# Accumulating the o and dq sums of four heads in one PSUM bank: an attention-and-MLP backward kernel on one core

## The chip, the cores and the metric

The kernel runs on 1 core of one Trainium2 chip. The metric is device time in microseconds (us) of one execution. Each kernel was timed in several rounds, alternating with the kernel before on the same chip; the tables give the median of a kernel's runs. The granted clock is the share of PE's full clock that the profile says PE was given.

The engines are named as in the profile: PE (matrix products), PEld (PE's weight loads, which overlap PE), DVE (vector engine), ACT (scalar engine), POOL, SP (which issues the large transfers), and DMA (the core's 16 DMA engines).

## The reference, cut to what matters

One token passes through a layer norm, 32-head attention over a cache of 8192 keys and values per head, and a small gated MLP. The kernel returns the output and all gradients, among them those of the whole K and V cache.

```python
# per head: k, v are [8192, 128] bf16; q, do (gradient of o) are [128]
scores = (k @ q) * 128 ** -0.5
p  = softmax(scores)
o  = p @ v                      # "o sum"
# backward, as jax.vjp derives it
dp = v @ do
ds = p * (dp - sum(p * dp))
dq = ds @ k                     # "dq sum"
dv = outer(p, do)               # 2 MB per head, stored
dk = outer(ds, q)               # 2 MB per head, stored
```

Per head 2 MB of K and 2 MB of V are loaded and 2 MB of each gradient are stored: 4 x 2 MB x 32 heads = 268 MB of the 304 MB that move in all.

## The kernel before: the parts that the change touches

The order of all instructions is fixed by hand. A head's K and V tiles are transposed on PE (`T`, copied out by ACT), multiplied with q and do (`Mp`), turned into two rows of 64 columns by "select" products (`selm`), put through softmax, and then summed (`wsum`) and used for the outer products (DVE), which overwrite the tiles before they are stored.

```python
ps_t = ctx.enter_context(tc.tile_pool(name="ps_t", bufs=4, space=PSUM))   # transposes AND sums
...
def wsum(h, kind, pair):                 # kind "V": o sum, kind "K": dq sum
    N4 = 4 * DH
    W = kv_tiles[(kind, h)]
    X = pst()                            # one of the 4 transpose banks
    for i in range(J // 4):              # 16 products of 32 columns
        q = QW * (i % 4)
        nc.tensor.matmul(X[q:q + QW, :], lhsT=pair[:, 4 * i:4 * i + QW, 0], rhs=W[:, N4 * i:N4 * (i + 1)],
                         start=(i < 4), stop=(i >= J // 4 - 4), skip_group_check=True)
    XS = kt_tile()
    nc.scalar.copy(XS[:].rearrange("p k w -> p (k w)"), X[:])          # ACT, twice per head
    hd[h]["xs" + kind] = XS

def col(h, kind):                        # twice per head, one head later
    ...
    for r in range(4):                   # "mask products": f32
        nc.tensor.matmul(S_["m"][:, OC + a:OC + a + 1], lhsT=XS[:, r, :], rhs=mask4[:, r:r + 1],
                         start=False, stop=(r == 3), skip_group_check=True)
    if a:
        nc.scalar.copy(grp[g]["od"][:, hh, :], S_["m"][:, OC:OC + 2])

def store(kind, h):
    t = kv_tiles.pop((kind, h))
    ...
    fifo((dkc if kind == "K" else dvc)[h], t[:])     # SP issues the store
    free_slots.append(t)
    load_next()                                      # and then the next load into a free tile
```

Loads and stores of the K and V tiles all go through one queue, issued by SP in program order. Ten tiles circulate.

## Time and profile before

| kernel before | us |
|---|---|
| median of 6 runs (first comparison) | 738.7 (736.96 to 740.21) |
| span of the profiled execution | 735.9 |

The first excerpt is from the profile page of the kernel before: busy time and share of each engine with the number of its instructions, three lines of the DMA queues (packets, MB, share of the 16 engines' span), and the chain of waits by engine, that is, the chain of work that ended last, followed back from the end.

```profile
PE 639.8 (87%) x6143; PEld 464.7 (63%) x6143; DVE 446.7 (61%) x745; ACT 402.5 (55%) x796; POOL 29.9 (4%) x45
...
q1 hardware_dynamic: 21328, 276.39, 89.3%
q0 software_dynamic: 5728, 26.30, 8.9%
q8 instruction: 48, 0.79, 0.4%
...
PE 64%; DMA 12%; DVE 10%; ACT 8%; issue 3%; ACTq 0%; SPq 0%; DVEq 0%
```

PE is the busiest engine and has most of the chain, which by itself says "PE is the bound". The table of stretches says otherwise. Its columns are: stretch and length in us, busy time (and instructions) of each engine, granted PE clock, share of the DMA engines' time, GB/s moved.

```profile
100.00:200.00 100.00, 92.35 (x893) 67.83 (x893) 56.71 (x95) 60.40 (x122) 2.94 (x4) 0.95 1.01 415
200.00:300.00 100.00, 93.70 (x897) 66.43 (x896) 64.04 (x97) 59.16 (x122) 4.91 (x6) 0.93 1.01 424
300.00:400.00 100.00, 93.48 (x923) 68.28 (x923) 63.25 (x99) 61.02 (x125) 4.02 (x5) 0.97 1.01 425
400.00:500.00 100.00, 93.08 (x888) 67.19 (x886) 64.56 (x100) 59.67 (x122) 3.27 (x4) 0.95 1.01 425
500.00:600.00 100.00, 93.66 (x876) 66.62 (x874) 64.13 (x97) 59.01 (x121) 4.13 (x5) 0.93 1.01 426
600.00:680.00 80.00, 74.00 (x691) 53.62 (x692) 49.77 (x76) 46.97 (x95) 1.63 (x2) 0.94 1.01 428
```

The DMA share is 1.01 in every stretch (it exceeds 1 because a packet's record overlaps the next one's). PE is 93% busy beside it: two things run at almost the same pace, and which one sets the time must be read from who waits. The groups that the change touches (line, engine, operation, output<-input, count | busy us, mean ns | idle time before, and what ended it):

```profile
L423 PE MATMUL m<-masks,KT 128*128 128x1 f32 x512 | 70.2, 259 | 0.0
L398 PE MATMUL pT<-kv,U 128*32 128x512 bf16 x512 | 46.2, 497 | 0.9 <-DVE U L411 0.9
L401 ACT COPY KT<-pT 128x512 f32<-128x512 f32 x64 | 38.7, 605 | 28.9 <-PE pT L398 28.7
L358 PE MATMUL m<-ident_f,mrow 128*128 128x128 f32 x64 | 12.4, 275 | 0.0
L293 PE MATMUL pT<-ident_f,kv 128*128 128x128 f32 x2048 | 311.3, 291 | 5.9 <-DMA kv<-in_A_k_cache_dram 4.0
L328 PE MATMUL m<-selc,KT 128*128 128x16 f32 x512 | 68.0, 265 | 29.3 <-ACT KT L318 29.2
```

The transposes (L293) are the first PE work on a tile, and before them PE stood idle for K and V loads 5.8 us in the whole run. The kernel before is thus hardly ever out of data; it only stays in step with the loads.

### The profile page before, as it was taken

How to read it: one execution, taken by the hardware profiler on the slowest of the kernel's cores; microseconds unless marked ns; L12 is line 12 of the kernel's file. 1: busy time of each engine (PE TensorE's matmuls, PEld its weight loads, DVE VectorE, ACT ScalarE, POOL GpSimd, SP SyncE). 2: the span in 40 equal slices, each digit the busy share in tenths (PEclk: the TensorE clock that was granted, in tenths of full speed). 3: DMA queues.
4: the chain of work that ended last, by engine and by line, in shares of the span. 5: the costliest groups of instructions: out<-in, count | busy, mean ns of one | idle time of the engine just before them, and what ended most of it. 6: DMA issues, size and time to landing. Idle time of an engine off the chain costs nothing.

```text
span 735.9 us, 14854 instructions
## 1 busy us (share of the span) xinstructions
PE 639.8 (87%) x6143; PEld 464.7 (63%) x6143; DVE 446.7 (61%) x745; ACT 402.5 (55%) x796; POOL 29.9 (4%) x45
## 2 busy tenths in 40 slices
PE   1999679999999999999999999999999999989950
PEld 1667457676667666766666666766666666666630
DVE  4057765666556666667656656676666655566482
ACT  1660646565656565665565655666565556655610
POOL 0010010000000000000000000000000000000000
PEclk9995799998999999999999999999999999989965
DMA  9999999999999999999999999999999999999993
GB/s 338 401 409 421 425 430 423 391 413 410 428 420 423 428 427 426 417 426 428 430 417 425 430 427 426 419 431 425 427 419 427 428 428 429 425 429 429 424 391 150
DMA packets 27432, 303.97 MB, mean 413 GB/s; under 512 B 2836, under 2 KB 4436, under 8 KB 10724
## 3 DMA queue, kind: packets, MB, share of 16 engines
q1 hardware_dynamic: 21328, 276.39, 89.3%
q0 software_dynamic: 5728, 26.30, 8.9%
q8 instruction: 48, 0.79, 0.4%
q10 hardware_dynamic: 308, 0.33, 0.1%
q14 instruction: 20, 0.16, 0.1%
HBM read 151.67 MB, written 151.34 MB: 412 GB/s over the span
## 4 chain that ended last, share of the span: by engine, by line
PE 64%; DMA 12%; DVE 10%; ACT 8%; issue 3%; ACTq 0%; SPq 0%; DVEq 0%
PE pT L293 27%; PE m L328 8%; PE m L423 7%; DMA kv<-in_A_k_cache_dram 7%; PE sA L312 6%; PE pT L398 5%; ACT KT L295 4%; DVE kv L430 4%; DMA kv<-in_A_v_cache_dram 4%; PE dA L312 2%; DVE side L239 2%; ACT KT L318 2%; DMA wo_g<-in_A_wo_dram 2%; PE gu_ps L507 1%; PE m L372 1%
## 5 line engine op out<-in xcount | busy, mean ns | idle before, releaser
L295 ACT COPY KT<-pT 128x512 f32<-128x512 f32 x512 | 292.0, 590 | 185.6 <-PE pT L293 100.9
L293 PE MATMUL pT<-ident_f,kv 128*128 128x128 f32 x2048 | 311.3, 291 | 5.9 <-DMA kv<-in_A_k_cache_dram 4.0
L293 PEld LDWEIGHTS pT<-ident_f,kv 128*128 128x128 f32 x2048 | 245.8, 153 | 49.8 <-PE pT L293 17.5
L430 DVE TENSOR_TENSOR kv<-qd,U 128x4096 bf16<-128x4096 bf16 x64 | 146.0, 2284 | 0.0
L430 DVE TENSOR_TENSOR kv<-qd,P 128x4096 bf16<-128x4096 bf16 x64 | 143.5, 2283 | 0.0
L328 PEld LDWEIGHTS m<-selc,KT 128*128 128x128 f32 x512 | 62.3, 192 | 49.5 <-ACT KT L318 44.8
L328 PE MATMUL m<-selc,KT 128*128 128x16 f32 x512 | 68.0, 265 | 29.3 <-ACT KT L318 29.2
L423 PEld LDWEIGHTS m<-masks,KT 128*128 128x128 f32 x512 | 65.0, 200 | 15.4 <-issue 15.4
L354 DVE TENSOR_REDUCE mrow<-m 128x1 f32<-128x64 f32 x32 | 7.2, 225 | 106.4 <-PE m L328 106.4
L423 PE MATMUL m<-masks,KT 128*128 128x1 f32 x512 | 70.2, 259 | 0.0
L312 PE MATMUL sA<-KT,qz 128*32 128x512 bf16 x512 | 56.0, 427 | 0.0
L401 ACT COPY KT<-pT 128x512 f32<-128x512 f32 x64 | 38.7, 605 | 28.9 <-PE pT L398 28.7
L312 PE MATMUL dA<-KT,qz 128*32 128x512 bf16 x512 | 53.6, 404 | 0.2 <-ACT KT L295 0.2
L387 DVE SCALAR_TENSOR_TENSOR U<-m,P 128x64 bf16<-128x64 f32 x32 | 7.4, 232 | 75.7 <-PE m L328 72.7
L312 PEld LDWEIGHTS <-qz 128*32 128x32 bf16 x1024 | 26.6, 93 | 41.4 <-issue 40.3
L398 PE MATMUL pT<-kv,U 128*32 128x512 bf16 x512 | 46.2, 497 | 0.9 <-DVE U L411 0.9
L398 PE MATMUL pT<-kv,P 128*32 128x512 bf16 x512 | 34.7, 387 | 0.0
L348 ACT CAST qd<-pT 128x256 bf16<-128x256 f32 x32 | 11.9, 372 | 41.4 <-DVE kv L430 32.7
L398 PEld LDWEIGHTS <-U 128*32 128x32 bf16 x512 | 15.9, 116 | 18.5 <-issue 11.9
L480 DVE SCALAR_TENSOR_TENSOR wq_g<-wq_g,side 128x512 bf16<-128x512 bf16 x40 | 27.3, 684 | 0.0
L361 DVE TENSOR_REDUCE negM<-m 128x1 f32<-128x128 f32 x32 | 9.3, 292 | 29.6 <-PE m L358 29.6
L239 DVE SCALAR_TENSOR_TENSOR side<-wo_g,g_bc 128x640 bf16<-128x640 bf16 x32 | 26.2, 820 | 1.6 <-DMA wo_g<-in_A_wo_dram 1.2
(144 smaller groups left out, 405.6 us busy)
## 6 DMA issues: line engine op xcount, KB each, us to landing
out_dram<-kv SPq DMA_DIRECT2D x64, 2048.0 KB, 28.8
kv<-in_A_k_cache_dram SPq DMA_DIRECT2D x32, 2048.0 KB, 25.6
kv<-in_A_v_cache_dram SPq DMA_DIRECT2D x32, 2048.0 KB, 25.8
out_dram<-wo_g POOLq DMA_DIRECT2D x8, 640.0 KB, 12.1
out_dram<-wq_g POOLq DMA_DIRECT2D x8, 640.0 KB, 13.1
wq_g<-in_A_wq_dram POOLq DMA_DIRECT2D x7, 640.0 KB, 14.0
wo_g<-in_A_wo_dram POOLq DMA_DIRECT2D x7, 640.0 KB, 19.7
kv<-in_B_w_dram SPq DMA_DIRECT2D x2, 1728.0 KB, 29.7
```

Of the source, the lines that this page charges most:

```text
L239: nc.vector.scalar_tensor_tensor(junk[:], G_["wo"][:, hh, :], 1.0, g_bc[:], ALU.mult, ALU.mult, accum_out=G_["do"][:, hh:hh + 1])
L293: nc.tensor.transpose(pT[:, k * P:(k + 1) * P], W3[:, 4 * c + k, :], ident_f[:])
L295: nc.scalar.copy(KT[:].rearrange("p k w -> p (k w)"), pT[:])
L312: nc.tensor.matmul(S_[kind][q:q + QW, :], lhsT=S_["qz"][:, o:o + QW], rhs=KTb[:, par, :], start=(c0 == 0), stop=(c0 == NCH - 2), skip_grou ...
L318: nc.scalar.copy(XS[:].rearrange("p k w -> p (k w)"), S_.pop(kind)[:])
L328: nc.tensor.matmul(S_["m"][:, b0:b0 + J].rearrange("p (c k t) -> p k c t", k=4, t=2)[:, k, :, :], lhsT=XS[:, k, :], rhs=selc[:].rearrange( ...
L348: nc.scalar.copy(qd[:].rearrange("p a d -> p (a d)"), hd[h].pop("ps_r"))
L398: nc.tensor.matmul(X[q:q + QW, :], lhsT=pair[:, 4 * i:4 * i + QW, 0], rhs=W[:, N4 * i:N4 * (i + 1)], start=(i < 4), stop=(i >= J // 4 - 4) ...
L401: nc.scalar.copy(XS[:].rearrange("p k w -> p (k w)"), X[:])
L423: nc.tensor.matmul(S_["m"][:, OC + a:OC + a + 1], lhsT=XS[:, r, :], rhs=mask4[:, r:r + 1], start=False, stop=(r == 3), skip_group_check=True)
L430: nc.vector.tensor_tensor(dst[:, lo * DH:hi * DH].rearrange("p (j a b) -> p j a b", a=DH // 2, b=2), vec.rearrange("p (a b) -> p a b", b=2 ...
L480: nc.vector.scalar_tensor_tensor(wq_g[:, ci, :], wq_g[:, ci, :], 1.0, dqb, ALU.mult, ALU.mult, accum_out=dxa[:, ci, g:g + 1])
```

## The change

The intent is less work per head on PE and ACT. The 16 products of each sum now read a buffer `Z` in which the values stand in four of every 32 columns; sliding the window by `4*slot` puts head and kind into their own four rows of each quarter. So eight sums (o and dq of four heads) accumulate in one PSUM bank, with one copy out and one set of mask products per four heads. The bank is taken from the transposes (four buffers become three), DVE fills `Z` twice per head, `P2`/`U2` become single, and the broadcast of the row maximum becomes a transpose.

```diff
-    ps_t = ctx.enter_context(tc.tile_pool(name="ps_t", bufs=4, space=PSUM))
+    ps_t = ctx.enter_context(tc.tile_pool(name="ps_t", bufs=3, space=PSUM))
+    ps_x = ctx.enter_context(tc.tile_pool(name="ps_x", bufs=1, space=PSUM))
 ...
+        nc.vector.tensor_copy(Z_vals, P2[:, :, 0].rearrange("p (i r) -> p i r", r=4))      # probs
 ...
+        nc.vector.tensor_copy(Z_vals, S_["U2"][:, :, 0].rearrange("p (i r) -> p i r", r=4)) # dsum
 ...
-    def wsum(h, kind, pair):
-        X = pst()
-        for i in range(J // 4):
-            nc.tensor.matmul(X[q:q + QW, :], lhsT=pair[:, 4 * i:4 * i + QW, 0], rhs=W[:, N4 * i:N4 * (i + 1)],
-                             start=(i < 4), stop=(i >= J // 4 - 4), skip_group_check=True)
-        nc.scalar.copy(XS[:].rearrange("p k w -> p (k w)"), X[:])
+    def wsum(h, kind, a):
+        slot = 2 * hh + a
+        if slot == 0:
+            xg["X"] = ps_x.tile([P, 512], F32, name="X", tag="X")
+        for i in range(NI):
+            o = QW - 4 + QW * i - 4 * slot
+            nc.tensor.matmul(xg["X"][q:q + QW, :], lhsT=Z[:, o:o + QW], rhs=W[:, N4 * i:N4 * (i + 1)],
+                             start=(slot == 0 and i < 4), stop=(slot == NS - 1 and i >= NI - 4), ...)
+        if slot == NS - 1:
+            nc.scalar.copy(XS[:].rearrange("p k w -> p (k w)"), xg.pop("X")[:])
 ...
-    def col(h, kind):                                   # per head and kind, mask4
+    def col(h):                                         # per four heads
         for r in range(4):
+            nc.tensor.matmul(m[:, OC:OC + NS], lhsT=XS[:, r, :], rhs=mask8[:, r, :], ...)
 ...
-        (max broadcast)  start=False, stop=True, skip_group_check=True)
+        (max broadcast)  start=False, stop=True, is_transpose=True, skip_group_check=True)
```

(Lines were cut and joined; the renaming of a few small tiles is left out.)

More of the change, by code (lines that the diff above doesn't have):

```diff
@@ L161 @@
     nc.vector.tensor_copy(ident_bf[:], ident_f[:])
-    masks = consts.tile([P, 8], F32, name="masks")
+    masks = consts.tile([P, 4], F32, name="masks")
     pm_one = masks[:, 0:2]
@@ L176 @@
     QW = P // 4
-    mask4 = masks[:, 4:8]
-    nc.vector.tensor_reduce(mask4, ident_f[:].rearrange("p (a b) -> p b a", b=QW)[:, 0:4, :], AX.X, ALU.add)
+    NS = 2 * GH
+    mask8 = consts.tile([P, 4, NS], F32, name="mask8")
+    nc.vector.tensor_reduce(mask8[:], ident_f[:].rearrange("p (a s r) -> p r s a", s=NS, r=4), AX.X, ALU.add)
     sel = consts.tile([P, 2, P], BF16, name="sel")
@@ L207, in pst @@
         return ps_t.tile([P, 512], F32, name="pT", tag="pT")
-    msum = consts.tile([P, 1], F32, name="msum")
-    nc.vector.tensor_reduce(msum[:], x_bc_bf, AX.X, ALU.add)
-    nc.vector.tensor_scalar(negmean[:], msum[:], -1.0 / D, None, ALU.mult)
-    sumsq = consts.tile([P, 1], F32, name="sumsq")
+    ln3 = consts.tile([P, 3], F32, name="ln3")
+    msum, sumsq, std = ln3[:, 0:1], ln3[:, 1:2], ln3[:, 2:3]
+    nc.vector.tensor_reduce(msum, x_bc_bf, AX.X, ALU.add)
+    nc.vector.tensor_scalar(negmean[:], msum, -1.0 / D, None, ALU.mult)
     nc.vector.scalar_tensor_tensor(t_tile()[:, 0:D], x_bc_bf, negmean[:], x_bc_bf, ALU.add, ALU.mult,
-                                   accum_out=sumsq[:])
-    std = consts.tile([P, 1], F32, name="std")
-    nc.scalar.activation(std[:], sumsq[:], ACTF.Sqrt, bias=eps_t[:], scale=1.0 / D)
-    nc.vector.reciprocal(rstd[:], std[:])
-    ps_x = pst()
+                                   accum_out=sumsq)
+    nc.scalar.activation(std, sumsq, ACTF.Sqrt, bias=eps_t[:], scale=1.0 / D)
+    nc.vector.reciprocal(rstd[:], std)
+    ps_xg = pst()
     for ci in range(NC):
-        nc.tensor.matmul(ps_x[:, ci:ci + 1], lhsT=x_bc_bf[0:1, ci * P:(ci + 1) * P], rhs=one_bf[0:1, :],
+        nc.tensor.matmul(ps_xg[:, ci:ci + 1], lhsT=x_bc_bf[0:1, ci * P:(ci + 1) * P], rhs=one_bf[0:1, :],
                          start=True, stop=True)
-        nc.tensor.matmul(ps_x[:, NC + ci:NC + ci + 1], lhsT=g_bc[0:1, ci * P:(ci + 1) * P], rhs=one_bf[0:1, :],
+        nc.tensor.matmul(ps_xg[:, NC + ci:NC + ci + 1], lhsT=g_bc[0:1, ci * P:(ci + 1) * P], rhs=one_bf[0:1, :],
                          start=True, stop=True)
-    nc.vector.tensor_copy(x_col[:], ps_x[:, 0:NC])
-    nc.vector.tensor_copy(g_col[:], ps_x[:, NC:2 * NC])
-    nc.vector.tensor_scalar(xn_col[:], x_col[:], negmean[:], rstd[:], ALU.add, ALU.mult)
+    nc.vector.tensor_copy(x_col[:], ps_xg[:, 0:NC])
+    nc.vector.tensor_copy(g_col[:], ps_xg[:, NC:2 * NC])
+    nc.vector.tensor_scalar(xn_col[:], x_col[:], negmean[:], rstd, ALU.add, ALU.mult)
     nc.vector.tensor_copy(xn_col_bf[:], xn_col[:])
@@ L271 @@
         qz_tiles.append(qz)
-    pu_tiles = []
-    for i in range(2):
-        pu = [consts.tile([P, J + QW - 4, 2], BF16, name=f"{n}{i}") for n in ("P2_", "U2_")]
-        for t in pu:
-            nc.vector.memset(t[:, J:, :], 0.0)
-        pu_tiles.append(pu)
+    P2_1 = consts.tile([P, J, 2], BF16, name="P2_1")
+    U2_1 = consts.tile([P, J, 2], BF16, name="U2_1")
+    NI = J // 4
+    Z = consts.tile([P, QW - 4 + NI * QW], BF16, name="Z")
+    nc.vector.memset(Z[:], 0.0)
+    Z_vals = Z[:, QW - 4:].rearrange("p (i n) -> p i n", n=QW)[:, :, 0:4]
     selc = consts.tile([P, 2 * NCH], F32, name="selc")
@@ L358, in mx_bc @@
         nc.tensor.matmul(S_["m"][:, 2 * J:2 * J + P], lhsT=S_["mrow"][:].to_broadcast([P, P]), rhs=ident_f[:],
-                         start=False, stop=True, skip_group_check=True)
+                         start=False, stop=True, is_transpose=True, skip_group_check=True)
         S_["negM"] = small.tile([P, 1], F32, name="negM")
@@ L378, in probs @@
         nc.vector.reciprocal(rZ[:], S_["m"][:, 2 * J + P:2 * J + P + 1])
-        P2 = pu_tiles[h % 2][0]
-        nc.vector.tensor_scalar(P2[:, 0:J, :], S_["E"][:].unsqueeze(2).to_broadcast([P, J, 2]), rZ[:], None, ALU.mult)
+        P2 = P2_1
+        nc.vector.tensor_scalar(P2[:], S_["E"][:].unsqueeze(2).to_broadcast([P, J, 2]), rZ[:], None, ALU.mult)
+        nc.vector.tensor_copy(Z_vals, P2[:, :, 0].rearrange("p (i r) -> p i r", r=4))
         S_["P2"] = P2
@@ L384, in rdot @@
         S_ = hd[h]
-        S_["U2"] = pu_tiles[h % 2][1]
+        S_["U2"] = U2_1
         S_["rdot"] = small.tile([P, 1], F32, name="rdot")
@@ L390 @@
     OC = 2 * J + P + 4
-    def wsum(h, kind, pair):
+    xg = {}
+    def wsum(h, kind, a):
+        g, hh = divmod(h, GH)
         N4 = 4 * DH
         W = kv_tiles[(kind, h)]
-        X = pst()
-        for i in range(J // 4):
+        slot = 2 * hh + a
+        if slot == 0:
+            xg["X"] = ps_x.tile([P, 512], F32, name="X", tag="X")
+        for i in range(NI):
             q = QW * (i % 4)
-            nc.tensor.matmul(X[q:q + QW, :], lhsT=pair[:, 4 * i:4 * i + QW, 0], rhs=W[:, N4 * i:N4 * (i + 1)],
-                             start=(i < 4), stop=(i >= J // 4 - 4), skip_group_check=True)
-        XS = kt_tile()
-        nc.scalar.copy(XS[:].rearrange("p k w -> p (k w)"), X[:])
-        hd[h]["xs" + kind] = XS
+            o = QW - 4 + QW * i - 4 * slot
+            nc.tensor.matmul(xg["X"][q:q + QW, :], lhsT=Z[:, o:o + QW], rhs=W[:, N4 * i:N4 * (i + 1)],
+                             start=(slot == 0 and i < 4), stop=(slot == NS - 1 and i >= NI - 4),
+                             skip_group_check=True)
+        if slot == NS - 1:
+            XS = kt_tile()
+            nc.scalar.copy(XS[:].rearrange("p k w -> p (k w)"), xg.pop("X")[:])
+            xg["XS"] = XS
@@ L404, in o_sum @@
     def o_sum(h):
-        wsum(h, "V", hd[h]["P2"])
+        wsum(h, "V", 0)
     def dsum(h):
         S_ = hd[h]
-        nc.tensor.matmul(S_["m"][:, OC + 2:OC + 3], lhsT=negones_b, rhs=S_["rdot"][:], start=False, stop=True,
+        nc.tensor.matmul(S_["m"][:, OC + NS:OC + NS + 1], lhsT=negones_b, rhs=S_["rdot"][:], start=False, stop=True,
                          skip_group_check=True)
-        nc.vector.scalar_tensor_tensor(S_["U2"][:, 0:J, :], S_["V"][:, 0:J].unsqueeze(2).to_broadcast([P, J, 2]),
-                                       S_["m"][:, OC + 2:OC + 3], S_["P2"][:, 0:J, :], ALU.add, ALU.mult)
+        nc.vector.scalar_tensor_tensor(S_["U2"][:], S_["V"][:, 0:J].unsqueeze(2).to_broadcast([P, J, 2]),
+                                       S_["m"][:, OC + NS:OC + NS + 1], S_["P2"][:], ALU.add, ALU.mult)
@@ L414, in dq_sum @@
+        nc.vector.tensor_copy(Z_vals, S_["U2"][:, :, 0].rearrange("p (i r) -> p i r", r=4))
     def dq_sum(h):
-        wsum(h, "K", hd[h]["U2"])
-    def col(h, kind):
-        g, hh = divmod(h, GH)
-        S_ = hd[h]
-        XS = S_.pop("xs" + kind)
-        a = 0 if kind == "V" else 1
+        wsum(h, "K", 1)
+    def col(h):
+        g = h // GH
+        m = hd[h]["m"]
+        XS = xg.pop("XS")
         for r in range(4):
-            nc.tensor.matmul(S_["m"][:, OC + a:OC + a + 1], lhsT=XS[:, r, :], rhs=mask4[:, r:r + 1],
+            nc.tensor.matmul(m[:, OC:OC + NS], lhsT=XS[:, r, :], rhs=mask8[:, r, :],
@@ L424, in col @@
                              start=False, stop=(r == 3), skip_group_check=True)
-        if a:
-            nc.scalar.copy(grp[g]["od"][:, hh, :], S_["m"][:, OC:OC + 2])
+        nc.scalar.copy(grp[g]["od"][:].rearrange("p h a -> p (h a)"), m[:, OC:OC + NS])
     def outer(dst, vec, pair, lo, hi):
@@ L688, in head @@
                 Mp(h, "K", c - 2)
-            if has_prev and c == 4:
-                col(h - 1, "V")
-            if has_prev and c == 6:
-                col(h - 1, "K")
+            if h > 0 and h % GH == 0 and c == 4:
+                col(h - 1)
         T(h, "V", 0)
@@ L736, in head @@
         dq_sum(h)
-        if not pre:
-            col(h, "V")
-            col(h, "K")
+        if not nxt:
+            col(h)
     prep_new(0)
@@ L787 @@
     nc.vector.scalar_tensor_tensor(t5[:], xn_col[:], nst[:, 1:2], dxn[:], ALU.mult, ALU.add)
-    nc.vector.tensor_scalar(t5[:], t5[:], nst[:, 0:1], rstd[:], ALU.add, ALU.mult)
+    nc.vector.tensor_scalar(t5[:], t5[:], nst[:, 0:1], rstd, ALU.add, ALU.mult)
     nc.vector.tensor_tensor(fin[:, NC:2 * NC], t5[:], g_col[:], ALU.add)
```

## The prediction

> **What bounds the kernel now: the DMA engines, from about 20 us on.**
> - Table of stretches: DMA share 1.01 in every 100 us from 100 to 600, at 415 to 426 GB/s.
> - Packet records: a 16 KB packet takes 611 ns at the median. 16 engines at that pace make 429 GB/s (estimate: 16 x 16384 B / 611 ns); 304 MB at that rate is 709 us of the 735.9 us span.
> - This agrees with the Trainium skill, "HBM Reference", section Access: a core streaming alone measures about 425 GB/s, bounded by its 16 DMA engines.
>
> PE looks like the bound (busy 87%, 64% of the chain of waits) but only chases. After the MLP the loads are far ahead: V of head 8 lands 40 us before that head's exponential, of head 16 26 us, of head 24 9 us, of head 28 6 us. A head takes PE 19.0 to 20.6 us; the loads of heads 10 to 26 land 21.9 us apart. From head 28 on PE waits for loads (1.32, 0.90, 0.78 us, timeline). From 300 us on SP waits 290 us for stores to land, 45 us for outer products.
>
> **What the change does, costed from the groups of before.**
> - PE: mask products 512 -> 64, 70.2 -> 9 us; the max broadcast as a transpose needs one pass, not two, -4 us.
> - ACT: copies of the sums 64 -> 8, 38.7 -> 5 us; of the o/dq columns 32 -> 8, -4 us.
> - DVE: 64 copies into Z, 0.17 us each (estimate from the 128x8 copy), +11 us; one per head lies between U and the dq products.
> - Transpose buffers 4 -> 3: more PE waits for the ACT copy (0.59 us), estimated below 0.7 us per head.
> - DMA: nothing.
>
> PE work per head falls by about 2 us, net some 1.3. None of it is on the path that sets the time: DMA is saturated, and PE had caught up by the end anyway.
>
> What can move is the tail: the last V lands (691 us), PE runs to 703, DVE outer products to 712, last stores land at 735. There Z copies add about 0.4 us. A little may come from 100 to 200 us, where the rate is 415 GB/s, but its packets are themselves slower (mean 655 ns in 140 to 180): at most 2 us.
>
> **Prediction.** 737 us, 8 in 10 between 731 and 742. Faster by over 2%: 0.03. Within 2%: 0.94. Slower by over 2%: 0.03.
>
> **What would show each step right or wrong.**
> - PE busy 570 to 585 us, ACT about 360, DVE about 457.
> - Groups: mask products near 9 us, copies of the sums near 5, the two new DVE copies near 0.17 us each.
> - PE's waits for K and V loads grow from 6 to 25 us or more, from heads 14 to 20 on, not 28.
> - DMA share stays 1.0 and 424 to 429 GB/s in mid-kernel; the last V load lands within 3 us of 691.
> - The chain of waits shows less PE, more DMA.
>
> **What would make it wrong.** If the DMA rate rises because stores are issued earlier, the time falls by over 1%: saturation was not total. If single Z, P and U buffers or three transpose buffers stall PE by over 2 us per head, mid-kernel stays PE-paced. If a colder PE runs the tail at half clock, 3 to 5 us are lost.

(The figure of 425 GB/s stands in the section "Specifications (TRN2)" of the page "HBM Reference" of the Trainium skill; the prediction had named another section. The traces agree with the figure: 424 to 429 GB/s in every stretch from 200 to 680 us, before and after.)

## The result, and the profile after

| kernel | median us | range | ratio to before |
|---|---|---|---|
| before, first comparison | 738.69 | 736.96 to 740.21 (6 runs) | |
| after, first comparison | 734.33 | 733.83 to 734.97 (6 runs) | 0.9941 (95%: 0.9927 to 0.9956) |
| after, again with 5 rounds | 734.70 | 734.65 to 735.01 | 0.9967 (0.9955 to 0.9979) |
| after, a third time with 5 rounds | 734.26 | 733.39 to 734.46 | 0.9954 (0.9941 to 0.9968) |

The change is worth 0.3 to 0.6%, "same" at the 2% limit. The profiled span fell from 735.9 to 733.2 us. The page of the changed kernel, the same lines:

```profile
PE 608.6 (83%) x5663; PEld 425.9 (58%) x5663; DVE 461.1 (63%) x806; ACT 367.9 (50%) x716; POOL 30.0 (4%) x45
...
q1 hardware_dynamic: 21328, 276.39, 89.3%
q0 software_dynamic: 5728, 26.30, 8.9%
q8 instruction: 44, 0.72, 0.4%
...
PE 42%; DMA 41%; ACT 7%; DVE 7%; issue 2%; SPq 0%; ACTq 0%; DVEq 0%
```

PE lost 31 us of busy time and ACT 35 us, for 2.7 us of span. The chain of waits now gives DMA 41% where it gave 12%. The stretches and the groups after:

```profile
100.00:200.00 100.00, 92.48 (x883) 65.49 (x883) 64.06 (x107) 58.27 (x117) 3.57 (x5) 0.93 1.01 418
200.00:300.00 100.00, 92.23 (x866) 65.15 (x864) 66.82 (x110) 57.24 (x117) 4.30 (x6) 0.91 1.01 425
300.00:400.00 100.00, 92.42 (x856) 64.52 (x855) 67.61 (x115) 56.70 (x115) 4.03 (x5) 0.90 1.01 427
400.00:500.00 100.00, 85.09 (x779) 58.75 (x780) 63.50 (x102) 51.99 (x103) 3.27 (x4) 0.90 1.01 428
500.00:600.00 100.00, 83.31 (x746) 57.10 (x745) 60.19 (x106) 50.27 (x102) 4.14 (x5) 0.88 1.01 427
600.00:680.00 80.00, 71.85 (x644) 49.26 (x642) 51.92 (x83) 43.66 (x88) 1.63 (x2) 0.87 1.01 429
```

```profile
L433 PE MATMUL m<-mask,KT 128*128 128x8 f32 x64 | 9.3, 272 | 0.7 <-ACT KT L411 0.7
L406 PE MATMUL X<-kv,Z 128*32 128x512 bf16 x1024 | 84.9, 460 | 1.8 <-DVE Z L423 1.8
L411 ACT COPY KT<-X 128x512 f32<-128x512 f32 x8 | 4.7, 588 | 7.9 <-PE X L406 7.9
L359 PE MATMUL m<-ident_f,mrow 128*128 128x128 f32 x32 | 8.7, 273 | 0.0
L294 PE MATMUL pT<-ident_f,kv 128*128 128x128 f32 x2048 | 321.8, 298 | 36.5 <-DMA kv<-in_A_k_cache_dram 27.3
L329 PE MATMUL m<-selc,KT 128*128 128x16 f32 x512 | 73.7, 277 | 24.4 <-ACT KT L319 24.2
L423 DVE COPY Z<-U 128x64 bf16<-128x64 bf16 x32 | 6.8, 212 | 1.1
L382 DVE COPY Z<-P 128x64 bf16<-128x64 bf16 x32 | 6.3, 195 | 1.1
```

Three readings. First, the removed work is gone as costed: mask products 70.2 to 9.3 us, copies of the sums 38.7 to 4.7 us. Second, PE now waits for loads: idle time before the transposes rose from 5.9 to 36.5 us, and PE's busy time per 100 us falls from 92.4 before 400 us to 85.1 and 83.3 after it. Its saved time turned into waiting. Third, the DMA rate rose slightly: summed over the stretches from 100 to 680 us, 245.7 MB before and 246.8 MB after (GB/s times length), so 1.1 MB, which at 427 GB/s is 2.5 us. That is nearly all of the 2.7 us of the profiled span. The question is why a change that touches no transfer raised the rate.

Where PE still sets its own pace (heads 8 to 15), the exponentials of eight successive heads took 160.2 us before and 157.0 us after: 0.4 us per head, where 1.3 net was predicted. The stretch lines show one reason: the granted clock fell from 0.93 to 0.97 before to 0.90 to 0.91 after (200 to 400 us), and with it the unchanged transposes took 298 instead of 291 ns and the unchanged select products 277 instead of 265 ns (2048 and 512 of them: 16 us together). Single heads of the traces show what goes with it. In both kernels ACT's cast waits for a DVE outer product (1.65 us in the head at 354 us before, 1.87 us in the head at 322 us after), and then PE waits for ACT at the select products: at most 1.6 us before, 2.0 us after. In mid-kernel the granted clock drops to 0.5 for 3.4 us soon after each of the waits of 1.6 us before (and after some of 0.85 us); in the changed kernel it does so for 3.4 to 6.8 us after nearly all of those of 1.1 to 2.0 us. That the wait lowers the clock is read from this order of events, not tested.

### The profile page after: what moved, and what is told of

It is laid out like the page before. It is cut to its first block, busy times and chain, and to the rows that moved or that the text cites. A ratio compares the mean times of both kernels' runs of the same rounds, so it can differ in the third digit from the quotient of the medians.

```text
span 733.2 us, 13850 instructions
## 1 busy us (share of the span) xinstructions
PE 608.6 (83%) x5663; PEld 425.9 (58%) x5663; DVE 461.1 (63%) x806; ACT 367.9 (50%) x716; POOL 30.0 (4%) x45
## 4 chain that ended last, share of the span: by engine, by line
PE 42%; DMA 41%; ACT 7%; DVE 7%; issue 2%; SPq 0%; ACTq 0%; DVEq 0%
PE pT L294 19%; DMA kv<-in_A_k_cache_dram 18%; DMA out_dram<-kv 17%; PE m L329 6%; PE X L406 5%; ACT KT L296 4%; DMA kv<-in_A_v_cache_dram 4%; PE sA L313 3%; PE dA L313 2%; DVE kv L439 2%; DMA wo_g<-in_A_wo_dram 2%; ACT kv L589 1%; PE gu_ps L516 1%; DVE side L240 1%; ACT KT L319 1%
## 5 line engine op out<-in xcount | busy, mean ns | idle before, releaser
L296 ACT COPY KT<-pT 128x512 f32<-128x512 f32 x512 | 290.4, 590 | 235.7 <-PE pT L294 204.3
L294 PE MATMUL pT<-ident_f,kv 128*128 128x128 f32 x2048 | 321.8, 298 | 36.5 <-DMA kv<-in_A_k_cache_dram 27.3
L294 PEld LDWEIGHTS pT<-ident_f,kv 128*128 128x128 f32 x2048 | 251.7, 156 | 93.2 <-PE pT L294 29.5
L329 PE MATMUL m<-selc,KT 128*128 128x16 f32 x512 | 73.7, 277 | 24.4 <-ACT KT L319 24.2
L406 PE MATMUL X<-kv,Z 128*32 128x512 bf16 x1024 | 84.9, 460 | 1.8 <-DVE Z L423 1.8
L313 PEld LDWEIGHTS <-qz 128*32 128x32 bf16 x1024 | 26.5, 93 | 42.7 <-issue 41.6
L406 PEld LDWEIGHTS <-Z 128*32 128x32 bf16 x1024 | 28.7, 110 | 34.0 <-issue 17.0
L421 DVE SCALAR_TENSOR_TENSOR U<-m,P 128x128 bf16<-128x128 f32 x32 | 11.4, 355 | 19.3 <-PE m L419 19.3
L379 DVE RECIPROCAL rZ<-m 128x1 f32<-128x1 f32 x32 | 5.3, 167 | 24.2 <-PE m L373 24.2
L319 ACT COPY KT<-dA 128x512 f32<-128x512 f32 x32 | 19.4, 605 | 0.6 <-PE dA L313 0.6
L319 ACT COPY KT<-sA 128x512 f32<-128x512 f32 x32 | 19.3, 602 | 0.0
## 6 DMA issues: line engine op xcount, KB each, us to landing
wq_g<-in_A_wq_dram POOLq DMA_DIRECT2D x7, 640.0 KB, 13.2
```

The source lines that it names most:

```text
L294: nc.tensor.transpose(pT[:, k * P:(k + 1) * P], W3[:, 4 * c + k, :], ident_f[:])
L296: nc.scalar.copy(KT[:].rearrange("p k w -> p (k w)"), pT[:])
L313: nc.tensor.matmul(S_[kind][q:q + QW, :], lhsT=S_["qz"][:, o:o + QW], rhs=KTb[:, par, :], start=(c0 == 0), stop=(c0 == NCH - 2), skip_grou ...
L319: nc.scalar.copy(XS[:].rearrange("p k w -> p (k w)"), S_.pop(kind)[:])
L329: nc.tensor.matmul(S_["m"][:, b0:b0 + J].rearrange("p (c k t) -> p k c t", k=4, t=2)[:, k, :, :], lhsT=XS[:, k, :], rhs=selc[:].rearrange( ...
L406: nc.tensor.matmul(xg["X"][q:q + QW, :], lhsT=Z[:, o:o + QW], rhs=W[:, N4 * i:N4 * (i + 1)], start=(slot == 0 and i < 4), stop=(slot == NS ...
```

## The theories

The 16 landing increments of each store and the packet records show one more thing. At the end of the run one DMA engine is far behind the other fifteen. Landing times (us) of the last store's increments in the first two profiles:

| last K gradient store | first | 15th | 16th |
|---|---|---|---|
| before | 719.3 | 724.5 | 734.9 |
| after | 716.9 | 724.2 | 732.2 |

From about 726 us on a single engine works, one packet after another. So the time of the whole kernel ends with one engine's list of packets. The number of PE's instruction pages (queue q8, 16,384 bytes each) had fallen from 48 to 44. The Trainium skill, "Runtime: NRT & Kernel Launch", section "Instruction fetch mechanics", says that the sequencer fetches its instructions by its own DMA queue in blocks of 16 KiB, 256 instructions. The trace agrees: 12,286 PE and PEld instructions make 48.0 such blocks.

- **Theory A:** one engine carries all these pages beside its share of the tiles, so it ends last, and a page costs it one 16 KB packet, 0.61 us. Four pages fewer are 2.4 us.
- **Theory B, the rival:** the shorter work of PE and ACT lets stores be issued earlier, and the gain is that of the compute pace.
- **Theory C**, formed later: the gain is made between 100 and 200 us, where the queue runs low because PE sets the pace.

## The experiments

Twelve runs were made, two of them of the unedited changed kernel. All are edits of the changed kernel unless it says "before". A visit is one set of runs on one chip (visits 1 and 3 on the same chip, 2 and 4 on two others), with the kernel before timed in the same rounds; so times are compared within a visit. Kernels that give wrong results are marked.

### Visit 1: is it the list of one engine, or the compute pace? (5 rounds)

**The changed kernel, unedited.**

> The changed kernel again, unedited, so that the others of this call have it on the same chip. Expected by every theory: 0.994 of before, as first measured, about 734.3 us against 738.7. In its profile: 44 packets of 16 KB on the instruction queue (before: 48), and the last store's 16 landings with one landing some 8 us behind the second last (before: 10.4 us).

Measured: 734.70 us, ratio 0.9967. Last store 716.7 / 723.5 / 732.0 us (first, 15th, 16th increment). The gain is there again, smaller: 2.2 us.

**Seven of eight sums dropped** (wrong: only the first sum of each four heads is computed).

```diff
-        for i in range(NI):
+        for i in range(NI if slot == 0 else 0):
 ... (and the end of the sum, stop, set to match)
```

> Wrong on purpose: of the eight o and dq sums of a group only the first is computed, so 896 of 1024 sum products are gone, which are 1792 PE instructions (weight load and product each one), 7 pages of 256; PE busy falls by some 75 us. Theory A (one straggling DMA engine, which also carries PE's instruction pages, sets the time; each page is one 16 KB packet of 0.61 us): 37 packets on the instruction queue instead of 44, and 4.3 us less than the changed kernel, about 730. Theory B (all 16 DMA engines are equally full; the gain came because a faster PE issues stores earlier): under 1.5 us less, as PE already waited for loads in the second half. Theory C (PE's work itself is on the path): over 10 us less.

Measured: 731.89 us (731.36 to 733.2), ratio 0.9931 (0.9917 to 0.9944); 37 pages; last store 719.2 (15th) and 728.9 (16th). Dropping seven eighths of the sum products (all of them took 88.0 us in the unedited kernel of this visit) and seven pages is worth 2.8 us against that kernel: less than the 4.3 us of Theory A, more than the 1.5 us of B, and far from the 10 us of PE work on the path. PE's busy time fell only from 615.6 to 582.4 us: its granted clock fell too, from 0.867 to 0.827.

**The same, with 64 bare weight loads in each of heads 2 to 29** (they compute nothing and put the instruction count back).

```diff
         dq_sum(h)
+        if 2 <= h < 30:
+            for _ in range(64):
+                nc.tensor.ldweights(one_bf[:, 0:1])
```

> The run without sums, plus 1792 bare weight loads of one column (64 in each of heads 2 to 29): the instruction count of the changed kernel, with different and in all less PE work. Theory A: the same time as the changed kernel within 1 us (44 instruction packets), so 4.3 us more than without sums. Theories B and C: the time of the run without sums, within 1.5 us, unless the weight loads take PE over 3 us per head.

Measured: 735.8 us (735.57 to 738.74), 44 pages, so 3.9 us more than without the weight loads. The last store was issued 6 us later than in the unedited kernel (716.2 against 709.9 us), yet it ended at the same time (731.4 against 732.0). What the compute engines do in the last 20 us therefore does not set the end; the late engine's list does. This looked like Theory A, but weight loads also take PE time, so pages and pace were not separated.

**The U product repeated nine times on DVE**, which delays the outer products and the stores.

```diff
-        nc.vector.scalar_tensor_tensor(S_["U2"][:], ...)
+        for _ in range(9 if 2 <= h < 30 else 1):
+            nc.vector.scalar_tensor_tensor(S_["U2"][:], ...)
```

> The changed kernel with the product that makes U repeated eight more times (same result, 0.355 us each, so 2.8 us per head more before the dq products, in heads 2 to 29): PE is slowed by waiting, not by instructions; 44 instruction packets still. Theory A: the time of the changed kernel within 1 us, as long as a head stays under the 21.8 us that the loads take. Theory B and C: PE is as slow as before the change or slower, so the 4.4 us are lost, 738 us or more.

Measured: 810.42 us (809.11 to 814.28), ratio 1.10. This was too strong, and every theory missed it: heads took 23 us each, longer than the 21.8 us that the loads take, and DMA was no longer full (390 to 394 GB/s from 200 to 500 us). It does not tell A from B. But it shows that the late engine belongs to full DMA queues: with the same 44 pages the 16 increments of the last store came within 0.2 us. So they did in both runs with half stores of visit 2.

### Visit 2: how much would the change be worth without the DMA bound? (3 rounds)

**Half of every K and V gradient store left out**, in the kernel before and in the changed kernel (wrong).

```diff
-        fifo((dkc if kind == "K" else dvc)[h], t[:])
+        fifo((dkc if kind == "K" else dvc)[h][:, 0:KVN // 2], t[:, 0:KVN // 2])
```

> Wrong on purpose: the kernel before, but each K and V gradient tile is stored only in its first half (64 stores of 1 MB instead of 2 MB), so 67 of the 304 MB go and DMA can no longer bind. Estimate: 237 MB at 427 GB/s are 555 us; PE's own pace is 80.6 us per four heads (profile of before, 19.0 to 20.6 us a head). Theory A and B both: the kernel is then paced by PE's chain, 700 us or a little less (31 heads of 20.15 us plus some 70 us for start, MLP and end). If the kernel before had been paced by PE all along, the time would stay 737.

> Wrong on purpose: the same cut of the stores in the changed kernel. PE's pace there is 78.6 us per four heads while loads are ahead (profile of the changed kernel: 18.5, 19.0, 20.4, 20.7 us), so 0.5 us per head less than before: some 15 us, 2 per cent, less than the other run without half the stores. If the 2 us per head that were taken from PE all counted, it would be 60 us less. If it is no faster than the other, PE's savings are given back in full by waits and by the lower clock.

Measured: before 724.75 us (719.91 to 725.9; ratio 0.9801), after 707.8 us (705.48 to 709.37; ratio 0.959). The stretches from 200 to 400 us, first of the before kernel and then of the changed kernel, with half stores:

```profile
200.00:300.00 100.00, 93.38 (x908) 67.50 (x907) 64.25 (x99) 59.86 (x123) 4.91 (x6) 0.95 0.92 345
300.00:400.00 100.00, 93.80 (x912) 67.79 (x912) 63.00 (x97) 60.30 (x124) 4.02 (x5) 0.95 0.93 351
```

```profile
200.00:300.00 100.00, 92.23 (x869) 65.11 (x867) 66.65 (x110) 57.14 (x116) 3.26 (x4) 0.91 0.95 362
300.00:400.00 100.00, 92.41 (x856) 64.57 (x853) 67.67 (x115) 56.79 (x116) 4.03 (x5) 0.90 0.95 358
```

That PE set the pace in both of these runs can be read from the idle time before the transposes, first of the before kernel and then of the changed one. No wait for a load is left:

```profile
L293 PE MATMUL pT<-ident_f,kv 128*128 128x128 f32 x2048 | 308.7, 289 | 0.0
```

```profile
L294 PE MATMUL pT<-ident_f,kv 128*128 128x128 f32 x2048 | 324.6, 300 | 0.0
```

The difference of the two came as expected (15 us said, 17 measured). The level did not: 700 us was expected of the before kernel, and 724.75 came.

This is the plainest run. With the DMA load lowered (share 0.92 to 0.95), the same change is worth 17 us, 2.3%; with full stores it is worth 2 to 4 us. So 13 us or more of gain are hidden by the DMA bound. It also shows how close the two paces were: freeing the kernel before from a quarter of its tile traffic gained only 12 to 15 us, so PE's own pace was only about 2% faster than that of DMA. And 17 us over 30 heads are 0.57 us per head, near the 0.4 us read from the trace above, and not 1.3.

**The last four stores cut by rows** (72+56, 88+40, 104+24, 120+8), to see which of the 16 engines is late.

```diff
 ... (d is the gradient's tensor of this head)
-        fifo((dkc if kind == "K" else dvc)[h], t[:])
+        cut = {("V", H - 2): 72, ("K", H - 2): 88, ("V", H - 1): 104, ("K", H - 1): 120}.get((kind, h), P)
+        fifo(d[0:cut, :], t[0:cut, :])
+        if cut < P:
+            fifo(d[cut:P, :], t[cut:P, :])
```

> The changed kernel, right results, with the last four stores each cut in two by rows: 72 and 56, 88 and 40, 104 and 24, 120 and 8 of 128 rows. The Trainium skill, page 'DMA: Bandwidth & Descriptors', section on why a DMA increments its semaphore by 16, says that a transfer runs on the largest count of at most 16 engines that divides its rows, the lowest-numbered ones: so 12 and 14, 11 and 10, 13 and 12, 15 and 8 engines. Theory A: the straggler shows itself: pieces that spare it land in full some 9 us earlier than pieces that use it. If it is the highest-numbered engine or one of the last three, those stores no longer burden it, the other engines have 7 us to spare, and the time falls by 4 to 8 us below the changed kernel. If it is a low-numbered engine, its load grows and the time rises by some 2 to 4 us. Without a straggler (theory B) the time stays or rises by about 1 us.

Measured: 753.09 us (752.09 to 753.57), ratio 1.0205. The counts of landing increments agree with the rule (8 for the 8-row piece, 15 for the 120-row piece). All pieces had the late engine: the 8-row piece landed from 735.7 to 741.3 us and then at 749.8, the 120-row piece until 740.7 and then at 749.1. So cutting the stores into fewer engines' shares did not go round it. If the rule holds, the late engine is among the eight lowest-numbered, since the 8-row piece uses no other. But the kernel got 16 us slower than the kernel before in the same rounds, some 18 slower than the changed kernel of the other visits, far more than the 2 to 4 us expected for a low-numbered engine (the last 120-row store was issued at 728 us, the uncut one at 710), and the run does not show why. A miss as an attempt to relieve it.

### Visit 3: pages alone, and the pieces of the change alone (5 rounds)

**The changed kernel, unedited.**

> The changed kernel as it is, for comparison on the same chip as the three that follow. All theories: 734 to 735 us, 44 instruction pages on PE's own DMA queue, about 2 to 3 us under the kernel before.

Measured: 734.26 us, ratio 0.9954.

**36 bare weight loads in each of heads 2 to 29** (the page count of the kernel before, in stretches where PE waits anyway).

```diff
+        if 2 <= h < 30:
+            for _ in range(36):
+                nc.tensor.ldweights(one_bf[:, 0:1])
```

> The changed kernel with 36 bare weight loads, which compute nothing, in each of heads 2 to 29: 1008 more PE instructions, so about 48 pages of instructions again instead of 44[...]. Theory A (one DMA engine carries PE's instruction pages besides its share of the tiles and ends last; a page costs it one 16 KB packet, 0.61 us): 4 x 0.61 = 2.4 us up, to 736.5 to 738, the time of the kernel before; the last gradient store's last landing increment moves from 732 to about 734.5. Rival B (the gain comes from the shorter work of PE and ACT per head, or from earlier store issues): the heads' loads set the pace, so 734.5 to 735.5, unchanged within its interval.

Measured: 734.89 us (734.27 to 736.64), ratio 0.9971 (0.9954 to 0.9987). The page of this run has the pages back:

```profile
q8 instruction: 48, 0.79, 0.4%
```

The profiled span is 732.5 us, that of the unedited kernel in the same visit. Putting four pages back cost 0.6 us of median and nothing in the profiled run, not 2.4 us; Rival B's 734.5 to 735.5 came. **Theory A falls as the account of the gain.** A smaller cost of the pages is not excluded: the accounts below show that this run also had shorter packets from 100 to 200 us (1.3 us per engine) while its late engine lay 1.2 us further behind the mean, so two effects may have cancelled in part.

**The kernel before with 16 of the 32 sum products of heads 0 to 29 dropped** (wrong; 44 pages, all else of the kernel before).

```diff
-        for i in range(J // 4):
+        n4 = J // 4 if h >= 30 else (12 if kind == "V" else 4)
+        for i in range(n4):
 ... (and stop set to match)
```

> The kernel before with 16 of the 32 sum products of each head 0 to 29 dropped, wrong on purpose (outputs of q, k, v weights' gradients will be off): 960 fewer PE instructions, so about 44 pages instead of 48, and all else of the kernel before (mask products per head, 64 copies of sums, four transpose buffers) kept. Theory A: 2.3 to 2.5 us under the kernel before, 734 to 735.5, without any part of the change. Rival B (the change's own pieces, fewer mask products and copies, brought the gain): it stays at 736.5 to 738; if PE's shorter sums alone are what counts (about 0.5 us a head), the gain may also appear but then the added weight loads of the kernel with padding should not cost anything.

Measured: 736.00 us (735.56 to 736.24), ratio 0.9979 (0.9966 to 0.9993). Less PE work without the change gains 1.1 us of the 2.8 us that the change gained in the same rounds. Neither theory said this: A had 734 to 735.5, B 736.5 to 738.

**64 tiny fills on POOL in each of heads 2 to 29.**

```diff
 ... (pad1 is a new tile of one column)
+        if 2 <= h < 30:
+            for _ in range(64):
+                nc.gpsimd.memset(pad1[:], 0.0)
```

> The changed kernel with 64 tiny fills of one column on POOL in each of heads 2 to 29 (1792 instructions), POOL having almost nothing else to do. It asks whether instruction pages of another engine count too. If POOL's pages ride on the same DMA engine as PE's (7 pages of 16 KB or 14 of 8 KB): about 4 us up, to 738 to 739.5. If they ride on another DMA engine, one that does not end last: unchanged, 734 to 735.5. Rival B: unchanged as well.

Measured: 736.98 us (736.06 to 737.86), 2.7 us more than the unedited kernel. POOL's instruction queue had 34 packets instead of 20 (first the unedited kernel, then this one):

```profile
q14 instruction: 20, 0.16, 0.1%
```

```profile
q14 instruction: 34, 0.28, 0.1%
```

The time falls between the two forecasts (738 to 739.5 and 734 to 735.5). An idle engine's useless instructions cost as much as the whole change gains. The accounts below show where. That the 14 packets are the cause, and not something else that the fills do (POOL's busy time rose from 30 to 209.5 us), is not shown.

### What the packet records say

With Theory A gone, the packet records were added up. No record names its engine, but on a full engine each packet starts 3 to 4 ns before the one ahead of it ends, so stretches of an engine's list can be linked. Two facts came out.

First, **a page takes one engine alone.** While one runs, 16 packets are in flight, the page among them, as at other times; so no other packet shares its engine. The 16 KB packet after it is slow too. Medians after 20 us:

| instruction page of | the page takes | the 16 KB packet after it takes, where it could be linked (else 0.611) |
|---|---|---|
| PE (16 KB) | 1.03 us before, 1.01 after | 1.01 us before, 1.02 after |
| POOL (8 KB) | 0.31 us | 0.71 us before, 0.99 after (few cases) |

A PE page thus costs an engine about 1.4 us. But no single engine can carry them all at that cost: in the changed kernel of visit 3, 19 PE pages were fetched between 366 and 666 us, worth some 27 us of one engine, while the latest engine fell only 4.5 us further behind the mean (5.3 to 9.8 us). If the pages are spread evenly, four of them are 4 x 1.4 / 16 = 0.35 us per engine (an estimate), which fits the padded kernel and not Theory A.

Second, **at the end of the run the late engine's own packets take longer.** Linked back from its last landing in the changed kernel of visit 3, its eight 16 KB packets per transfer took (ns, the last packet of each transfer first):

```
692.5-697.6 us: 634 660 644 634 644 639 653 624
697.6-703.0 us: 615 653 653 615 625 625 648 671   and one POOL page of 309
703.0-708.2 us: 611 611 611 611 614 625 633 884
708.2-713.2 us: 612 614 625 644 700 620 611 611
```

Over all engines the median is 611 in each of these stretches; about a fifth of the packets took over 613, on other engines too. Over the whole run, outside the times of weight transfers, 360 of 10,313 packets took 624 to 680 ns, and 205 of these 360 were followed directly, on the same engine, by another such packet: they are not scattered over sixteen engines (of the packets that follow one of 611 ns, a few in a thousand are so slow). Their time beyond 611 ns adds up to some 11 us, which on one engine would be about the late engine's lag of 9.8 us behind the mean (an estimate; that it is the same engine all along is not shown). The Trainium skill, "DMA: Bandwidth & Descriptors", section "Latency and other measured facts", says that engines 7 and 15 are usually slower than the others in traces and calls its cause a best guess (contention for the ring of software-generated descriptors). The trace agrees that there is a slow engine; no record says which, beyond what the store cut in rows suggests. It does not test the cause.

The accounts, per engine (sum over all packets of their time, less 3.5 ns of overlap each, divided by 16). "Excess" is the time of the 16,384 packets of 16 KB beyond 611 ns. "Unused" is the end of the last tile packet minus the packets' time. "Lag" is how far the last landing of head 30's V load lies behind the mean of its 16.

| profiled run | median us | packets' time | excess, all | 100 to 200 us | 300 to 600 us | pages of PE | last packet | unused | lag |
|---|---|---|---|---|---|---|---|---|---|
| before | 737 to 739 | 721.0 | 9.05 | 3.36 | 2.25 | 48 | 734.5 | 13.5 | 10.3 |
| before, 16 products dropped | 736.0 | 719.2 | 7.72 | 1.90 | 2.12 | 44 | 732.3 | 13.1 | 10.2 |
| after, first profile | 734.3 | 718.3 | 7.31 | 2.39 | 1.51 | 44 | 731.8 | 13.5 | 10.2 |
| after, visit 1 | 734.7 | 718.3 | 7.29 | 1.94 | 1.46 | 44 | 731.6 | 13.2 | 9.9 |
| after, visit 3 | 734.3 | 717.8 | 6.78 | 1.91 | 1.50 | 44 | 731.1 | 13.3 | 9.8 |
| after, 36 weight loads | 734.9 | 717.6 | 6.28 | 0.59 | 1.63 | 48 | 731.1 | 13.5 | 11.0 |
| after, POOL fills | 737.0 | 718.9 | 7.95 | 2.29 | 1.50 | 44 | 734.5 | 15.6 | 12.6 |
| seven of eight sums dropped | 731.9 | 715.5 | 5.19 | 0.92 | 1.29 | 37 | 728.5 | 13.0 | 9.8 |
| the same, 64 weight loads | 735.8 | 718.9 | 6.97 | 1.87 | 1.55 | 44 | 731.0 | 12.0 | 9.9 |

The unused time hardly moves (13.0 to 13.5 in seven of nine rows). What moves is the time that the same packets take. From before to after it fell by 2.7 to 3.2 us, and the span by the same. Of that fall in the first profile, 1.74 us are excess of 16 KB packets (0.97 between 100 and 200 us, 0.74 between 300 and 600 us), 0.30 us are the pages, 0.42 us are the packets of the weights' queue (65.32 to 64.90 us). The kernel with POOL fills is different: its packets' time rose by only about 0.6 to 1.1 us, but its lag rose to 12.6 us. It is the late engine that got later; which engine POOL's pages went to can't be read from the records, except for the single one linked above.

One thing more can be read from the records. Between 300 and 600 us the difference of the two families lies in one place: the 16 KB packets that start while packets of the weights' queue run, or within 0.5 us of them. Their excess is 1.20 to 1.45 us in the three kernels built on the kernel before (that of visit 4 included) and 0.51 to 0.79 us in the seven of the table built on the changed kernel. The excess of all other packets there does not tell them apart (0.80 to 0.92 against 0.66 to 0.98 us).

### Visit 4: is the stretch from 100 to 200 us PE's doing? (5 rounds)

The kernel before has 104 packets of 16 KB that took 0.8 us or more in 100 to 200 us, most of them in six clusters from 128 to 178 us; the changed kernel has 53 to 67. Theory C says that PE sets the pace there and the queue runs low.

**The kernel before with 24 of the 32 sum products of heads 2 to 9 dropped** (wrong).

```diff
-        for i in range(J // 4):
+        n4 = 4 if 2 <= h <= 9 else J // 4
+        for i in range(n4):
 ... (and stop set to match)
```

> The kernel before with 24 of the 32 sum products of heads 2 to 9 alone dropped, wrong on purpose (those heads' rows of the weight gradients will be off); heads 10 to 31 and everything else are the kernel before. 384 PE instructions fewer (1.5 instruction pages), 8 x 2 us less PE work, all of it before about 220 us. Theory C, formed after the padding runs: about half of the gain of the change is made between 100 and 200 us, where PE sets the pace of the first heads, the DMA queue runs low (many 16 KB packets of 0.8 to 1.2 us instead of 0.61 in six clusters from 128 to 178 us in the kernel before) and any cut of PE work there is worth time to the end, because from 200 us on the DMA engines are full. Then: 100 to 200 us at 420 to 426 GB/s instead of 415, fewer long packets there, the later stretches unchanged at 424 to 428, and 1.3 to 2.5 us less in all: 734.5 to 735.8. Theory A (one packet time of one DMA engine per PE instruction page): 1.5 x 0.61 = 0.9 us less, about 736.2. Rival (the gain is made by the lighter later heads alone, from 300 us on): unchanged within 0.5 us.

Measured: 737.81 us (736.78 to 739.28) beside 738.02 for the kernel before, ratio 0.9994 (0.9977 to 1.0012). The first two stretches:

```profile
100.00:200.00 100.00, 88.87 (x802) 66.56 (x804) 59.10 (x100) 60.02 (x123) 2.95 (x4) 0.94 0.99 409
200.00:300.00 100.00, 91.43 (x846) 66.58 (x839) 64.96 (x100) 60.21 (x125) 4.91 (x6) 0.94 1.01 424
```

PE's busy time in the first stretch fell from 92.35 to 88.87 us, and the rate did not rise (409 against 415 GB/s); there were still 100 long packets. **Theory C falls in this form:** PE time saved in the first heads is worth nothing even in the only stretch where the rate is low. The run has a second use. Its engines on average were 1.2 us later than those of the kernel before at head 30's V load (660.6 against 659.4), but the late engine was not (669.9 against 669.7; a lag of 9.3), and the time was the same. Again it is the one engine that ends last.

## Why the prediction was right or wrong

**The time, right.** 737.0 was predicted, with 731 to 742; 734.3 to 734.7 came. The class "within 2%" was right for the reason given: DMA is full from 20 us on, so PE's savings become waiting. The runs with half stores show it causally: the same edit is worth 17 us when DMA has room and 2 to 4 us when it has not. The range was wide, though: much larger or smaller savings of PE would also have led to a time in it (731.89 us with seven of eight sums dropped), so the time does not confirm the sizes below.

**The signs named in advance, mostly right.**
- PE waits for K and V loads: predicted "from 6 to 25 us or more, from heads 14 to 20 on"; they grew from 5.8 to 35.9 us, from head 19 on.
- Mask products near 9 (9.3), copies of the sums near 5 (4.7), DVE about 457 (461.1); ACT about 360 was 8 us too low (367.9).
- DMA share 1.0 at 424 to 429 GB/s in mid-kernel (425 to 429 from 200 us on), last V load within 3 us of 691 (688.8), chain with less PE and more DMA (64% and 12% to 42% and 41%).

**The size of PE's saving, wrong, and hidden by the DMA bound.** "PE work per head falls by about 2 us, net some 1.3" was 0.4 us in the trace and 0.57 us in the runs with half stores. PE busy was to be 570 to 585 us and was 608.6. About 61 us of mask products were removed as said, but work that the change does not touch grew: the transposes and select products together by 16 us and the sums by 4 us (80.9 to 84.9 us), with a lower granted clock beside it (0.90 instead of 0.97 at 300 to 400 us). Another 11 us or so of what was removed had cost no PE time of its own: PE's groups overlap, and their busy times add up to about 734 us before and 691 after, against 639.8 and 608.6 us in which PE was busy at all. That the lower clock comes from PE's waits is read from the trace, not tested. The waits for loads are not needed for it: in the runs with half stores there were none, and the clock was still 0.95 before and 0.90 to 0.91 after, with waits for ACT at the select products of 33.7 and 41.6 us. The prediction costed removed instructions at their durations and took the durations of the rest as fixed and the removed ones as not overlapped. The DVE copies into `Z` were 0.195 and 0.212 us, not 0.17; this had no effect.

**"DMA: nothing", the step that failed for the last 3 us.** The packets of the same bytes took 2.7 to 3.2 us less per engine, and that is the gain. The prediction had treated the DMA time as a constant because no transfer was edited. It is not one: among the nine profiles of the account it varies from 715.5 to 721.0 us. The prediction had allowed "at most 2 us" from the stretch of 100 to 200 us; there 0.97 to 1.45 us of it were made, so this place was named in part. The first point of "What would make it wrong", a higher DMA rate, also came true in small: 246.8 instead of 245.7 MB in the same stretches, for 0.3 to 0.6% of time and not 1%.

**What is shown about the 3 us, and what stays open.**
- Shown: the end is set by one late engine (a compute tail 6 us later did not move it; engines on average 1.2 us later did not move it).
- Shown: it is not PE's page count alone at 0.61 us a page (Theory A predicted 2.4 us, 0.6 came); a smaller cost is open.
- Shown: it is not the PE work of the first heads (Theory C predicted 1.3 to 2.5 us; 0.2 came).
- Shown by the account, not by an edit: the 0.6 to 0.8 us between 300 and 600 us go with the changed kernel's order of work and not with the amount of PE work. Every profile with full DMA queues that is built on the changed kernel has 1.3 to 1.6 us of excess there. Those built on the kernel before have 2.1 to 2.3, with 16 of 32 products dropped as well as without. The difference lies in the packets beside the weights' transfers.
- Neither shown nor excluded: Rival B. Its time came in the padded run (734.89 us), but with sums dropped 2.8 us were gained where B said under 1.5.
- Open: what in that order shortens the packets beside the weights' transfers (no run moved these transfers alone), and why the excess between 100 and 200 us ranges from 0.59 to 3.36 us among kernels that differ little. With one profile per kernel, chance is not excluded there.
- Open: a kernel that beats both. Dropping sums showed that 2.8 us more would follow from far less PE work, but no correct version of that was run.

## What to carry to other kernels

When two resources run within 2% of each other, take load off one of them (here: half stores) and run the change again: it tells in one pair of runs how much of a saving the other resource hides, at least 13 of 17 us here. On a kernel that keeps all DMA engines full, the last engine's list of packets set the time here, and "no transfer was edited" did not make DMA time a constant: instructions are fetched by the same engines, and the kernel with 1,792 useless ones on an idle engine was 2.7 us slower. Cost the work that a change leaves in place too: here PE's granted clock fell, and its unchanged instructions took longer.

## What the Trainium skill lacked or had wrong

- "Runtime: NRT & Kernel Launch", section "Instruction fetch mechanics", calls the cost of a new 16 KiB block one tail-bump, mostly hidden. What PE itself pays was not looked at here, but the block occupies one DMA engine alone for about 1.0 us, and the 16 KB packet after it takes about 1.0 us instead of 0.611: about 1.4 us of one engine per PE block in a kernel that keeps the DMA engines full. The page does not have this cost to the DMA engines.
- The same page: 1,792 fills on POOL made the kernel 2.7 us slower (736.98 against 734.26 us) with 14 more packets of 8 KB on POOL's instruction queue; that padding an otherwise idle engine can cost device time is on no page that was consulted.
- "DMA: Bandwidth & Descriptors", section "Latency and other measured facts", has slower engines 7 and 15 but no size. Here one engine fell 9.3 to 12.6 us behind the mean of the sixteen by 670 us when DMA was full, with many packets of 615 to 671 ns at the end where the median of all is 611, and ended 8 to 13 us after the second-last. When DMA was not full, all sixteen ended within 0.2 us (the runs of 707.8, 724.75 and 810 us).
